# Routed rows fetched and written back by transfers with an address from the index, in a gated mix of a long convolution and a two-row expert

## The chip, the cores and the metric

The kernel runs on one core of one Trainium2 chip. The core has five engines, each with its own instruction stream: TensorE (PE in the profile: matrix products and transposes, results in PSUM), VectorE (DVE), ScalarE (ACT: activation functions, and copies out of PSUM), GpSimd (POOL) and SyncE (SP, which here only issues transfers). Transfers run on 16 DMA engines. Engines wait for each other through semaphores. The metric is the device time of one execution in microseconds (us), the median of several runs.

## What is computed

The input `u` has 2048 tokens of 512 bf16 channels. Two branches are computed from it and mixed per token with a gate.

```
g = sigmoid((u * gate_w).sum(-1))                 # one gate for each token
# branch a: diagonal state-space convolution, one causal filter of 2048 taps for each channel
K[d, l] = Re( sum_n C[d,n] * exp(dt[d] * A[d,n] * l) * dt[d] * B[d,n] ),   l rounded to bf16
a = causal_conv(u, K) + u * Dskip                 # reference: FFT of length 4096
# branch b: the two tokens with the largest router value go through a gated expert
r   = u @ w_r
idx = argsort(-r)[:2]
y   = (silu(u[idx] @ w_gate) * (u[idx] @ w_up)) @ w_down * sigmoid(r[idx])    # 512 -> 1792 -> 512
b   = u;  b[idx] += y
out = g * a + (1 - g) * b
```

Rounding the lag `l` to bf16 makes runs of neighbouring taps equal, so only a few hundred distinct exponents are needed for each channel; a few taps at the two ends of the blocks fall out of this scheme ("edge rows") and are added separately: eight output rows, each a product of taps and a few input rows (tokens 0 to 3, 1024 and 1025).

## The kernel before

Everything is written against one large SBUF array `AR` and four PSUM tensors `ps`; the profile shows these names only. The channels are handled in two halves of 256 (`h` = 0, 1), the tokens in two blocks of 1024.

Stages, in the order in which the program declares them:

- Loads: a constant table `c_bf` (identity matrices first), the parameters, `u` in eight pieces (`U`), the forward matrices `c_fwd`, small constants (`c_rev` is a 128x128 reversal matrix `RV`), the expert's gate and up weights (`WG`, `WU`).
- `scaled`, `trig`, `turns`, `tab1`, `tab2`: tables of complex exponentials, built from products of few direct exponentials and sines (ScalarE for exp and sin, TensorE for the angle steps, L696 to L710; VectorE for the products, L459).
- `routing` (L793 on): transposes `u` (L803), folds the blocks for the forward transform (`fold`, L789), computes gate and router values (`lg`, L819), and finds the two best tokens by two rounds of a maximum over each partition, a TensorE transpose and a maximum across (`gmax`, L848 and L852). This gives a one-hot matrix `OHT` and the token numbers `IDX`. The expert follows: `gat` collects the two rows out of `U` by 64 matmuls with the one-hot matrix (L878) into `XS`; `xed` collects the edge rows with four matmuls against a 0/1 matrix at the end of the constant table (L886) into `XE`; then `ffn1` (L899, gate and up), SiLU, `dn` (L912) and `ytr` (L919), a scaling into `ZB`, and an indirect transfer with accumulation issued by GpSimd (L923) that adds the two rows to `out` in HBM.
- `copies` (two HBM to HBM copies of `u` to `out`, ahead of that scatter), and `reload`, which reads `out` back into `U`: this is `b`.
- `forward` (L954), `kgen` (L973 to L1000: filter taps; its last step multiplies edge taps with `XE` into `ZB`), `kspec` (L1025: filter spectrum, with its matrices `c_ksp`; the second part is seeded either by ScalarE, L1018, or by two matmuls, L1016), `products` (VectorE), `inverse` (L1113), then the scaling and the stores of `out`.

The order is not the order of declaration. `ORDER` is one written-out sequence of all operations; each engine's stream is that sequence restricted to it, and SyncE's transfers are in it too, so a transfer whose wait is not over holds back every transfer behind it in SyncE's stream. `SECOND` says for each operation that may run on two engines (most evictions from PSUM, `EV`, and scalings, `SCL`: ScalarE or VectorE; one step of `trig`, L684; the seed of `kspec`) which one takes it. `PLACES` gives the PSUM banks and SBUF slots. Waits are worked out from what operations read and write. Buffers share memory: the down weights `WD` lie over the transposed `XT`, the filter matrices `KP` over the forward matrices and folded blocks.

The steps named below stand at these lines of the kernel before:

```
gat   L878   64 matmuls 128x2           xed  L886   4 matmuls 40x512
ffn1  L899   2 x 56 matmuls             dn   L912   56 matmuls          ytr  L919
L463  the scaling of the expert's output into ZB;  L923  the scatter;  L931  a clearing that GpSimd does later
L474, L478   EV and SCL;   L684  the int32 step of trig;   L481  every issue of a transfer on SyncE
```

Of the kernel before, what the change touches and what calls it, by code (L numbers as in the profile page):

```python
# [348 lines left out]
EROWS = edge_rows()  # L349
NE = len(EROWS)  # L350
ETB = sorted({PLACE[s][0] for _, _, src in EROWS for s in src})
ERT = sorted({PLACE[t][0] for t, _, _ in EROWS})
EK0 = 256
ECOL = 512
EW = 32 + NE


def small_mats():
    eye = np.eye(128)
    xs = np.zeros((128, len(ETB), EW))  # L360
    ek = np.zeros((128, 4, 2, 32))
    oh = np.zeros((NE, len(ERT) * 128))
    for r, (t, k, src) in enumerate(EROWS):
        for s in src:
            tb, p = PLACE[s]
            xs[p, ETB.index(tb), 32 + r] = 1.0
        for c4 in range(4):
            ek[c4, c4, k, r] = 1.0
        tb, p = PLACE[t]
        oh[r, ERT.index(tb) * 128 + p] = 1.0  # L370
    return np.concatenate([eye, -eye, ek.reshape(128, -1), xs.reshape(128, -1)], 1), oh
# [4 lines left out]
    "02101c01l01h01o00200000101k00300500401j00u00700v00w00600y01201w01u01y00q00h00b00x01301f00z01101g01400n01x00a01000g01m00k02h01p02f01702p06t01v01501t02n"  # L376
    "00902i01800l01901s02d01i02g02q00802o02b01a02z01b00o02e06r02702802c02r00e02j02k02306s00f02l01z03002s02002601e00c01d01r02502m00m03103201q02t05f033034022"
    "05e02u06q00j03509k03e03f02404l06u03g00d03603h03y05h05g05i03i03j09l00s00p03k06v04k03l06w03v03m03n05x05j05w01605k03o03p05l03704m03z03q06x03r01n04500i076"
    "03s07705m02v06y03t07904n02w04o03u03w07007104306z00t07805y04q07b07a07204p05q04r04402907c07307d05r02y07404703x07504s05s02x0b40b304t0b505t04807e04004u04b"
    "0b20b604904a04v07f04d0b705u04e06004104w04c07g0b807h05z06107p0500420ba07j04f0bc05v04x0b906i00r04y0bi06h07k05104g0bd05406j04h0bj07n04i0bl07q05204z07i053"  # L380
    "07o06k07s06l06o06n04607r05505707u05n05607y0bb06p05o05806m05905p0bk05a05b0690bn0be06e06f06g05c06806207w06306a0bf0bm0bg05d06b09m06c06409n06607m06d07t07l"
    "02a0bh08409q07v09o07z03807x0bp0650800bo08109r0c108309p03b06708509t08908208708608a09u0bq09s0br09v08808b08c08d09w03c0bs08e08g08i0bt0bv08f08j0bw0a008l09x"
    "0bz09y08h08x08k08m0a108n0c208y0bu04j0a208v08o08q0a308p08w09z0bx08s08r0a408z0a70by0900a80c308t0a90c40910c60aa0ca0ab0a509c0c00a609a09d09b0ac09h0c508u092"
    "09e09f09g0ad0c70cc0cb0cd0ce09i0930cf0c80cg0c90ci09j0cj0ch0ck0940cm0al0cl0cn0cp0co0cq0cr0cs0am0390950cu0da0db0an03d0cx0ap0ao0960cv0cy0ct0aq0dc0cw0970cz"
    "0980ar0990d00d20d10d40d30d503a0e60de0h10af0ae0d60df0h00e50dg0dh0d70dl0dd0e20do0dm0ag0di0dj0h20dp0dq0dn0dv0fe0dk0ai0dw0d90fg0dr0ds0dt0ah0dx0ff0ak0fj0d8"
    "0fk0e30e40aj0du0as0fh0fp0gy0dz0e10fl0ea0at0eg0e00eo0dy0ge0fi0e70au0e90gz0ep0ev0eh0ee0e80ec0eb0fn0gb0aw0ei0av0fm0gc0gd0ef0gf0ax0et0fo0ay0az0gg0ed0gk0g7"
    "0ey0ej0gj0fq0b10g90ga0eq0es0gi0er0ew0ek0eu0f00ex0g80f10fs0gh0fr0b00ez0f40f80el0ft0f60f50f90em0gp0f70fv0f20gq0fu0gl0en0gr0f30fw0h40fd0fx0gm0fy0gn0fc0h7"
    "0h50gx0h60fa0gs0fb0fz0gv0g00h80ha0gw0g10g30h30h90hb0g20hj0g40hn0g50go0g60hc0ho0hd0he0hk0hl0gu0hp0gt0hm0hf0hg0hq0ht0hu0hh0hr0hi0hs"
)
SECOND = (  # L390
    "000000000000000000000000000000000000000000010000000000000000000000000000000000000000100010001010001000000000100000000000000000000000000000000000000000"
    "000000000000000000001000000100000000000001000000000000000000000000000000000000000000000000001001010000000000000000000000000000000000000000000000000000"
    "000000000000000000000000000000010000001000000000000000000000000000000000000000000000000000000000000000010000000100000000000000000000000000000000000000"
    "000000000000000000000000000000000000100100000010010000000000000000000000000000000000000000000000000000000000000000000000000000000000000000000000000000"
    "0000000000000000000000000000000000000000000"
)
PLACES = (
    "02465433161002423232540160245222227767777201014646000422440404000146624264456404442240101000000000006260260223046640004012343160264022020752457"
# [4 lines left out]
def bass_gated_mix__ssm_conv_s4__moe_arch_mod__prompt_kernel(nc, A_u, A_A_re, A_A_im, A_B_re, A_B_im, A_C_re, A_C_im, A_log_dt, A_Dskip,  # L403
# [9 lines left out]
    rv_c = const(np.eye(128)[::-1], "c_rev")  # L413
# [15 lines left out]
    with ExitStack() as es:  # L429
# [132 lines left out]
        DQ([(CB(0, 128, 0, (1, 256)), cb_c[:, 0:256])], [], [(CB, "i")], 65536)  # L562
# [13 lines left out]
        DQ([(RV(0, 128, 0, (1, 128)), rv_c[:, :])], [], [RV], 32768)  # L576
        DQ([(CF(0, 128, 0, (1, 160)), cf_c[:, :])], [], [CF], 81920)
        DQ([(CB(0, 128, 256, (1, CBW - 256)), cb_c[:, 256:])], [], [(CB, "o")], 196608)
# [10 lines left out]
        TT(DG(0, 128, 0, (128, 4), (1, 128)), CB(0, 128, 0, (0, 4), (1, 128)), DTP(0, 128, 0, (1, 4), (0, 128)), ALU.mult, [CBI, DTP], [DG])  # L589
        AL = psum(2)  # L590
# [205 lines left out]
        def routing():  # L796
# [26 lines left out]
            b = misc()  # L823
            def od(h):
                for par, w in ((0, CB), (1, RV)):
                    r = h.matmul(b(0, 128, 2 * par, (4, 8), (1, 2)), w(0, 128, 0, (1, 128)), SGB(0, 128, 64 + 2 * par, (4, 8), (1, 2)), start=par == 0, stop=par == 1, skip_group_check=True)
                return r
            P.op(PE, od, [(SGB, "p"), CBI, RV], [b], cost=0.06)
            EV(SGB(0, 128, 0, (1, 32)), b(0, 128, 0, (1, 32)), [b.buf], [(SGB, "s")])
# [43 lines left out]
            gb = misc()  # L873
            def gat(h):
                last = None
                for db in range(4):
                    for tb in range(16):
                        last = h.matmul(gb(0, 128, db * 2, (1, 2)), U(0, 128, tb * D + db * 128, (1, 128)), OHT(0, 128, tb * 2, (1, 2)), start=(tb == 0), stop=(tb == 15))  # L878
                return last
            P.op(PE, gat, uk(*range(16)) + [OHT], [gb.buf], cost=64 * 0.0252)  # L880
            EV(XS(0, 128, 0, (1, 8)), gb(0, 128, 0, (1, 8)), [gb.buf], [XS])
            xe = misc()
            def xed(h):
                last = None
                for i, tb in enumerate(ETB):
                    last = h.matmul(xe(0, EW, 0, (1, D)), CB(0, 128, ECOL + i * EW, (1, EW)), U(0, 128, tb * D, (1, D)), start=(i == 0), stop=(i == len(ETB) - 1))  # L886
# [330 lines left out]
```

## Time and profile before

| | |
|---|---|
| median of 3 runs | 149.09 us (148.96 to 149.79) |
| profiled execution | 149.01 us, its span 147.2 us |
| TensorE busy | 139.8 us (95%) |
| VectorE busy | 137.5 us (93%) |
| ScalarE busy | 126.0 us (86%) |
| GpSimd busy | 23.8 us (16%) |
| granted TensorE clock | 1.00 |

The span is the time from the first to the last thing in the trace of one profiled execution; the execution's own time is 1.8 us longer. A line of a page or an answer names the line of the kernel, the engine, the operation, the tiles written and read, and the count; then busy time, mean duration in ns, and the idle time of the engine just ahead of these instructions with what ended it. Durations overlap a little: the next instruction of VectorE or ScalarE begins some 0.07 to 0.1 us before the end of the one ahead. The chain of waits follows back from the last instruction what released it. SPq is SyncE's sequencer, which issues transfers.

### The profile page before, as it was taken

To read this page: it belongs to the slowest core of one execution; us is meant where nothing else is said; L and a number is where in the kernel's file an instruction comes from. 1 tells how busy PE (TensorE), PEld (TensorE's weight loads), DVE (VectorE), ACT (ScalarE), POOL (GpSimd) and SP (SyncE) were. 2 spreads that over 40 slices of the span, in tenths; PEclk is the share of its full clock that TensorE was granted. 3 is DMA by queue.
4 is the path that set the end of the run, shared out by engine and by line. 5 is a ranking of instruction groups with operands and counts; after the bars stand their busy time and mean duration, and the time that the engine had idled before them with its cause. 6 is when DMAs were issued, how large, how long until landed. Compare 5 with 4: busy or idle time off the path is not lost.

```text
span 147.2 us, 4010 instructions
## 1 busy us (share of the span) xinstructions
PE 139.8 (95%) x1731; PEld 102.1 (69%) x1731; DVE 137.5 (93%) x192; ACT 126.0 (86%) x203; POOL 23.8 (16%) x11
## 2 busy tenths in 40 slices
PE   7999999999999999999899999999999999799990
PEld 2766754677564445589768899977866888688870
DVE  0699998999999999999999999999999999999982
ACT  4699999999999999999899999998889998079220
POOL 3001000000000899999000001000000000000000
PEclk9999999999999999999999999999999999999999
DMA  4999999169100000059300006689200004004404
GB/s 121 276 367 298 412 407 558 44 220 533 40 4 0 0 4 0 0 179 414 129 0 4 0 0 206 230 245 390 85 0 4 2 2 143 0 4 140 120 25 143
DMA packets 12787, 21.16 MB, mean 144 GB/s; under 512 B 1207, under 2 KB 8386, under 8 KB 12610
## 3 DMA queue, kind: packets, MB, share of 16 engines
q1 hardware_dynamic: 11762, 20.26, 38.8%
q10 hardware_dynamic: 976, 0.66, 1.5%
q8 instruction: 13, 0.21, 0.6%
q14 instruction: 4, 0.03, 0.1%
q0 software_dynamic: 32, 0.00, 0.0%
HBM read 18.81 MB, written 4.20 MB: 156 GB/s over the span
## 4 chain that ended last, share of the span: by engine, by line
DVE 51%; PE 42%; issue 2%; DMA 2%; SPq 0%; DVEq 0%
DVE AR L459 45%; PE ps L954 19%; PE ps L973 6%; PE ps L705 3%; DVE AR L466 2%; PE ps L899 2%; PE ps L710 2%; DVE AR L474 2%; DMA AR<-c_bf 2%; DVE AR L621 1%; PE ps L1113 1%; PE ps L699 1%; PE ps L878 1%; PE ps L819 1%; PE ps L789 1%
## 5 line engine op out<-in xcount | busy, mean ns | idle before, releaser
L459 DVE TENSOR_TENSOR AR<-AR 128x2048 bf16<-128x2048 bf16 (+7 forms) x133 | 115.5, 927 | 3.5 <-DMA AR<-c_bf 2.8
L474 ACT ACTIVATE AR<-ps 128x1024 bf16<-128x1024 f32 (+6 forms) x66 | 52.6, 833 | 3.1 <-PE ps L1025 2.4
L1113 PE MATMUL ps<-AR 128*128 128x256 bf16 x256 | 29.5, 273 | 0.9 <-DVE AR L459 0.8
L470 ACT ACTIVATE AR<-ps 128x1024 bf16<-128x1024 int16 (+2 forms) x34 | 28.4, 882 | 2.0 <-PE ps L598 1.9
L954 PE MATMUL ps<-AR 128*128 128x512 bf16 x128 | 29.9, 379 | 0.0
L1113 PEld LDWEIGHTS ps<-AR 128*128 128x128 bf16 x256 | 24.5, 98 | 5.2 <-DVE AR L459 2.0
L923 POOL DMA_INDIRECT out_dram<-AR x1 | 21.5, 21527 | 33.9 <-DVE AR L459 33.9
L954 PEld LDWEIGHTS ps<-AR 128*128 128x128 bf16 x128 | 12.1, 97 | 13.6 <-ACT AR L474 0.5
L973 PEld LDWEIGHTS ps<-AR 128*128 128x128 bf16 x512 | 18.6, 96 | 1.8 <-issue 0.5
L973 PE MATMUL ps<-AR 128*128 128x84 bf16 (+1 forms) x512 | 19.0, 196 | 0.4 <-issue 0.4
L1025 PE MATMUL ps<-AR 128*128 128x256 bf16 x160 | 19.3, 273 | 0.1
L1025 PEld LDWEIGHTS ps<-AR 128*128 128x128 bf16 x160 | 15.3, 98 | 4.1 <-DVE AR L459 0.6
L478 ACT ACTIVATE AR<-AR 128x256 int32<-128x256 f32 (+3 forms) x29 | 16.1, 582 | 0.1
L1123 ACT ACTIVATE AR<-ps,AR 128x256 bf16<-128x256 f32 x24 | 10.0, 478 | 4.9 <-PE ps L1113 4.7
L470 ACT ACTIVATE ps<-AR 128x256 f32<-128x256 bf16 x26 | 11.4, 484 | 0.0
L470 ACT ACTIVATE AR<-AR 128x1024 bf16<-128x1024 int16 (+4 forms) x12 | 9.4, 783 | 0.4 <-DVE AR L684 0.3
L646 PE MATMUL ps<-AR 128*128 128x464 bf16 x22 | 6.9, 446 | 0.9 <-DVE AR L649 0.9
L459 DVE TENSOR_TENSOR AR<-AR,ps 128x2048 bf16<-128x2048 bf16 (+1 forms) x6 | 7.2, 1229 | 0.0
L705 PE MATMUL ps<-AR 128*128 128x512 f16 x24 | 6.2, 379 | 0.0
L1135 ACT ACTIVATE AR<-ps,AR 128x256 bf16<-128x256 f32 x2 | 0.9, 474 | 4.8 <-PE ps L1113 4.7
L710 PE MATMUL ps<-AR 128*128 128x512 bf16 x16 | 4.8, 381 | 0.0
L803 PE MATMUL ps<-AR 128*128 128x128 bf16 x64 | 4.4, 219 | 0.3 <-DMA AR<-c_rev 0.2
(76 smaller groups left out, 99.5 us busy)
## 6 DMA issues: line engine op xcount, KB each, us to landing
AR<-c_ksp SPq DMA_DIRECT2D x5, 512.0 KB, 6.1
AR<-in_A_u_dram SPq DMA_DIRECT2D x8, 256.0 KB, 4.8
AR<-out_dram SPq DMA_DIRECT2D x4, 512.0 KB, 4.8
AR<-c_inv SPq DMA_DIRECT2D x1, 2048.0 KB, 8.7
AR<-in_B_w_gate_dram SPq DMA_DIRECT2D x1, 1792.0 KB, 11.6
AR<-in_B_w_up_dram SPq DMA_DIRECT2D x1, 1792.0 KB, 15.2
out_dram<-AR SPq DMA_DIRECT2D x14, 128.0 KB, 2.2
AR<-c_fwd SPq DMA_DIRECT2D x4, 256.0 KB, 6.2
```

Of the source, the lines that this page charges most:

```text
L459: return P.op(DVE, lambda h: h.tensor_tensor(out=o, in0=a, in1=b, op=op), rd, wr, cost=tt_cost(o, a, b), **k)
L470: return P.op(ACT, lambda h: h.activation(out=o, in_=a, func=func, scale=scale, bias=bias), rd, wr, cost=0.185 + nel(o) * 0.833e-3 + (0.09 ...
L474: return P.op((ACT, DVE), (lambda h: h.activation(out=o, in_=a, func=ACTF.Copy), lambda h: h.tensor_copy(o, a)), rd, wr, cost=(0.185 + n * ...
L478: return P.op((ACT, DVE), (lambda h: h.activation(out=o, in_=a, func=ACTF.Copy, scale=c), lambda h: h.tensor_scalar(out=o, in0=a, scalar1= ...
L705: r = hh.matmul(pb(0, 128, b * 512, (1, 512)), TI(4), PC(0, 128, k * D + h * HC, (0, 2), (1, HC)), start=False, stop=True, skip_group_chec ...
L710: r = hh.matmul(pb(0, 128, b * 512, (1, 512)), CB(0, 128, 128 * sign, (1, 128)), TOFF(1), start=False, stop=True, skip_group_check=True)
L923: P.op(POOL, lambda h: h.indirect_dma_start(dr(out, 0, (D, L), (1, D)), bass.IndirectOffsetOnAxis(ap=IDX(0, 2, 0, (1, 1)), axis=0), ZB(0, ...
L954: last = h.matmul(pb(0, 128, j * 512, (1, 512)), F[ft](0, 128, (kt * 2 + 1 - j) * 128, (1, 128)), pm[q](0, 128, kt * 512, (1, 512)), start ...
L973: last = hh.matmul(pb(0, 128, g // k * 512 + g % k * W4 + o, (1, n)), TP[h][1 - i // 2](0, 128, (b0 + g) * 128, (1, 128)), r[i](0, 128, (b ...
L1025: last = hh.matmul(pb(0, 128, n * 256, (1, 256)), KP[u](0, 128, tau * 128, (1, 128)), KC[h](0, 128, jg * 256, (1, 256)), start=(k == 0 and ...
L1113: r = hh.matmul(pb(0, 128, e * 256, (1, 256)), G(0, 128, ((par * 2 + part) * 4 + ft) * 512 + (2 * t2 + e) * 128, (1, 128)), X(0, 128, h * ...
L1123: return [hh.activation(out=U(0, 128, tb * D + h * HC, (1, HC)), in_=pb(0, 128, tb // 2 % 2 * 256, (1, HC)), func=ACTF.Copy, scale=SG(0, 1 ...
```

## The change

- The routed rows are no longer collected by matmuls. When `IDX` is there, SyncE reads each token number from SBUF into a register and issues two transfers from `u` in HBM whose address comes from it: one puts the row as a column pattern into `XS` (128 partitions, 4 values of 2 bytes each), one puts it as a row into `XE`. `gat` and its eviction are gone.
- The expert's output is scaled and added to the fetched row in one VectorE instruction, and SyncE writes the two finished rows to `out` by two transfers with an address from the register, instead of the accumulating scatter on GpSimd. They wait for the two copies, as the scatter did.
- The edge rows' inputs are loaded straight from `u` into `XE` by two small transfers; `xed` and its eviction are gone. There is now one row for each pair of kind and source, and the 0/1 matrix `c_oh` adds up where several sources belong to one output row.
- The reversal matrix is no longer loaded; VectorE copies the identity with its columns read backwards.
- `ORDER`, `SECOND` and `PLACES` are new. Counted over whole streams: TensorE loses `gat` and `xed` and one pair of seed matmuls (ScalarE takes that seed); VectorE gains the reversal copy, has two more 128x256 scalings (ScalarE two fewer), and hands the one int32 step of `trig` it had and one 128x8 eviction to ScalarE. In SyncE's stream the first half of the down weights now stands ahead of the up weights; the fetch stands between the up weights and the second half of the down weights; both copies stand behind that; the row writes stand behind the first filter load, four others behind them; the rest of the constant table is loaded among the filter loads. The first half of the down weights waits for TensorE to finish with `XT`, as before.

```diff
-    xs = np.zeros((128, len(ETB), EW))
     ek = np.zeros((128, 4, 2, 32))
     oh = np.zeros((NE, len(ERT) * 128))
-    for r, (t, k, src) in enumerate(EROWS):
-        for s in src:
-            tb, p = PLACE[s]
-            xs[p, ETB.index(tb), 32 + r] = 1.0
+    for r, (k, _) in enumerate(ESRC):
         for c4 in range(4):
             ek[c4, c4, k, r] = 1.0
+    for t, k, src in EROWS:
         tb, p = PLACE[t]
-        oh[r, ERT.index(tb) * 128 + p] = 1.0
+        for q in src:
+            oh[ESRC.index((k, q)), ERT.index(tb) * 128 + p] += 1.0
...
-        DQ([(RV(0, 128, 0, (1, 128)), rv_c[:, :])], [], [RV], 32768)
...
+        assert ESRC == [(0, 0), (0, 1), (0, BLK), (0, BLK + 1)] + [(1, i) for i in range(4)]
+        for r, src in ((0, ((BLK * D, 2), (D, 2))), (4, ((D, 4),))):
+            DQ([(XE(32 + r, 4, 0, (1, D)), dr(A_u, 0, *src, (1, D)))], [], [(XE, r)], 4096)
...
+        CP(RV(0, 128, 0, (1, 128)), CB(0, 128, 127, (-1, 128)), [CBI], [RV])
...
-            gb = misc()
-            def gat(h):
-                last = None
-                for db in range(4):
-                    for tb in range(16):
-                        last = h.matmul(gb(0, 128, db * 2, (1, 2)), U(0, 128, tb * D + db * 128, (1, 128)), OHT(0, 128, tb * 2, (1, 2)), start=(tb == 0), stop=(tb == 15))
-                return last
-            P.op(PE, gat, uk(*range(16)) + [OHT], [gb.buf], cost=64 * 0.0252)
-            EV(XS(0, 128, 0, (1, 8)), gb(0, 128, 0, (1, 8)), [gb.buf], [XS])
-            xe = misc()
-            def xed(h):
-                last = None
-                for i, tb in enumerate(ETB):
-                    last = h.matmul(xe(0, EW, 0, (1, D)), CB(0, 128, ECOL + i * EW, (1, EW)), U(0, 128, tb * D, (1, D)), start=(i == 0), stop=(i == len(ETB) - 1))
-                return last
-            P.op(PE, xed, uk(*ETB) + [(CB, "o")], [xe.buf], cost=len(ETB) * 0.22)
-            EV(XE(32, NE, 0, (1, D)), xe(32, NE, 0, (1, D)), [xe.buf], [XE])
+            def row(c):
+                return nc.values_load(IDX(c, 1, 0, (1, 1)), engines=[mybir.EngineType.SP], min_val=0, max_val=L - 1, skip_runtime_bounds_check_because="4096 less a match in the table 4096 - token")
+            def gath(h):
+                r = []
+                for c in range(2):
+                    x = A_u[0, bass.ds(row(c), 1), :]
+                    r.append(h.dma_start(XS(0, 128, c, (2, 4)), x.rearrange("o (k p) -> p (o k)", p=128), allow_slow_non_contiguous=True))
+                    r.append(h.dma_start(XE(c, 1, 0, (1, D)), x))
+                return r
+            P.op(SP, gath, [IDX], [XS, (XE, "x")], cost=4.0, n=4, nbytes=1200000, dma=True)
...
-            TS(ZB(0, 2, 0, (1, D)), yt(0, 2, 0, (1, D)), RTS(0, 2, 37, (1, 1)), MUL, [yt, K("rs"), (ZB, None)], [(ZB, "y")])
-            P.op(POOL, lambda h: h.indirect_dma_start(dr(out, 0, (D, L), (1, D)), bass.IndirectOffsetOnAxis(ap=IDX(0, 2, 0, (1, 1)), axis=0), ZB(0, 2, 0, (1, D)), None, compute_op=ADD),
-                 [(ZB, "y"), IDX], [DX], cost=1.5, nbytes=2048, dma=True)
+            STT(ZB(0, 2, 0, (1, D)), yt(0, 2, 0, (1, D)), RTS(0, 2, 37, (1, 1)), XE(0, 2, 0, (1, D)), MUL, ADD, [yt, K("rs"), (ZB, None), (XE, "x")], [(ZB, "y")])
+            P.op(SP, lambda h: [h.dma_start(out[0, bass.ds(row(c), 1), :], ZB(c, 1, 0, (1, D))) for c in range(2)], [(ZB, "y"), IDX], [DX], cost=3.0, n=2, nbytes=2048, dma=True)
```

More of the change, by code (lines that the diff above doesn't have):

```diff
@@ L349 @@
 EROWS = edge_rows()
-NE = len(EROWS)
-ETB = sorted({PLACE[s][0] for _, _, src in EROWS for s in src})
+ESRC = sorted({(k, s) for _, k, src in EROWS for s in src})
+NE = len(ESRC)
 ERT = sorted({PLACE[t][0] for t, _, _ in EROWS})
@@ L379 @@
[L379 to L382, printed above, removed]
@@ new lines @@
+    "000000000000000000010000001000000100000000000000000000000000000000000000000000000000000000001000100000001000000000000000000000000000000000000000000000"
+    "000000000000000000000000000100000000000010000000000000000000000000000000000000000000000000000000011000100000001000000000000000000000000000000000000000"
+    "000000000000000000000000000000000001000000000100100000000000000000000000000000000000000000000000000000000000000000000000000000000000000000000000000000"
+    "000000000010000000000000000000000000000000"
```

46 lines of the change are left out of this document (22 added, 24 removed).

## The prediction

> **What bounds the kernel now.** I read the page's busy shares, then the same engines by stage, then VectorE's waits, then the chain of work in order of time. (In all rows L numbers are lines of the kernel before.)
>
> ```profile
> PE 139.8 (95%) x1731; PEld 102.1 (69%) x1731; DVE 137.5 (93%) x192; ACT 126.0 (86%) x203; POOL 23.8 (16%) x11
> ```
> ```profile
> 3.62:14.40 10.78, 9.97 (x115) 7.39 (x113) 9.55 (x16) 9.38 (x15) 0.55 (x2) 1.00 0.98 312
> 14.40:73.86 59.46, 59.01 (x781) 37.25 (x782) 58.34 (x103) 58.36 (x88) 21.54 (x2) 1.00 0.48 184
> 73.86:139.47 65.61, 64.37 (x798) 53.43 (x799) 65.31 (x65) 55.80 (x99) 0.52 (x1) 1.00 0.26 88
> ```
> ```profile
> DVE AR L464 <- PE ps L598: 1.1, 1, 1.1
> DVE AR L848 <- PE ps L852: 0.6, 2, 0.3
> DVE AR L459 <- PE ps L973: 0.4, 1, 0.4
> ```
>
> (Columns: stretch, its length, busy time of TensorE, of its weight loads, of VectorE, ScalarE and GpSimd, granted clock, DMA share, GB/s.) Three engines are full at once between 14.40 and 73.86: TensorE idles 0.45 us, VectorE 1.12, ScalarE 1.10. From 73.86 to 139.47 VectorE alone is full (0.30 idle) and ScalarE has 9.8 to spare. So VectorE, from 3.62 on, is the line that everything hangs on. A change can win only by shortening VectorE's work or by removing its idle time, 1.23 + 1.12 + 0.30 = 2.65 us before the tail, most of which is waits on TensorE: 1.1 at the start, 0.6 in the routing reductions, 0.4 before the first filter half. The 21.5 us that GpSimd spends in the scatter are on no path: its next user, the reload, is issued at 88.38.
>
> The profiled run took 149.01 us with a span of 147.2, so 1.8 lie outside; the median of the runs, 149.09, is 0.08 above it.
>
> **The change, part by part.** First the stretch of TensorE's order in which the routed rows are handled, then VectorE and ScalarE by shape, the queue, and the transfers' time to landing.
>
> ```profile
> 16.25 1.58 PE ps L819 x64
> 17.83 0.89 PE ps L954 x4
> ...
> 27.02 0.97 PE ps L886 x4
> ...
> 29.73 1.58 PE ps L878 x64
> ...
> 33.06 1.38 PE ps L899 x56
> ```
> ```profile
> 19.21 0.17 DVE L848 TENSOR_REDUCE AR<-AR 128x1 f32<-128x16 bf16 x1
> 33.86 0.13 DVE L464 TENSOR_SCALAR AR<-AR 2x1 int32<-2x1 f32 x1
> ```
> ```profile
> L459 DVE TENSOR_TENSOR AR<-AR 128x2048 bf16<-128x2048 bf16 x22 | 26.5, 1214 | 0.1
> L459 DVE TENSOR_TENSOR AR<-AR 128x1792 bf16<-128x1792 bf16 x18 | 19.2, 1079 | 0.0
> L459 DVE TENSOR_TENSOR AR<-AR 128x512 bf16<-128x512 bf16 x21 | 8.3, 422 | 2.8 <-DMA AR<-c_bf 2.8
> L459 DVE TENSOR_TENSOR AR<-AR,ps 128x2048 bf16<-128x2048 bf16 x4 | 4.8, 1234 | 0.0
> L684 DVE TENSOR_SCALAR AR<-AR 128x1024 int32<-128x1024 int32 x1 | 0.7, 674 | 0.0
> L478 DVE TENSOR_SCALAR AR<-AR 128x256 int32<-128x256 f32 x2 | 0.6, 314 | 0.0
> L463 DVE TENSOR_SCALAR AR<-ps,AR 2x512 bf16<-2x512 bf16 x1 | 0.5, 466 | 0.0
> L466 DVE SCALAR_TENSOR_TENSOR AR<-ps,AR 128x512 f32<-128x512 f32 x1 | 0.7, 692 | 0.0
> L474 DVE COPY AR<-ps 128x8 bf16<-128x8 bf16 x1 | 0.2, 205 | 0.0
> L459 DVE TENSOR_TENSOR AR<-AR 128x256 bf16<-128x256 bf16 x4 | 1.0, 273 | 0.0
> ```
> ```profile
> L684 ACT ACTIVATE AR<-AR 128x1024 int32<-128x1024 int32 x3 | 3.1, 1049 | 0.0
> L478 ACT ACTIVATE AR<-AR 128x256 int32<-128x256 f32 x14 | 5.4, 426 | 0.0
> L474 ACT ACTIVATE AR<-ps 8x512 bf16<-8x512 f32 x1 | 0.6, 588 | 0.0
> ```
> ```profile
> 62.89 2.45 SPq L481 DMA_DIRECT2D AR<-c_ksp  x5
> 88.38 1.88 SPq L481 DMA_DIRECT2D AR<-out_dram  x3
> ```
> ```profile
> AR<-in_B_w_up_dram SPq DMA_DIRECT2D x1, 1792.0 KB, 15.2
> AR<-in_B_w_down_dram SPq DMA_DIRECT2D x1, 768.0 KB, 8.4
> AR<-c_bf SPq DMA_DIRECT2D x1, 104.0 KB, 11.4
> out_dram<-in_A_u_dram SPq DMA_DIRECT2D x2, 13.3
> AR<-in_A_log_dt_dram SPq DMA_DIRECT2D x1, 1.0 KB, 2.2
> ```
> ```profile
> q1 hardware_dynamic: 11762, 20.26, 38.8%
> ```
>
> *TensorE.* Out go the gather of the routed rows (L878, 1.58) and of the edge rows (L886, 0.97): 2.55 us, all in the full stretch. (One pair of carry matmuls, later, goes to ScalarE; it has 9.8 us free there: nothing.)
>
> *VectorE's work.* Out: the 128x1024 int32 step (0.674, now ScalarE's), the 128x8 copy (0.205), the 2x512 scaling (0.466). In: two 128x256 scalings taken from ScalarE (0.314 each, the second in bf16 and bounded by the same row) and a 2x512 multiply-add with a row from PSUM (nearest row 0.692). 1.345 out, 1.320 in: nothing. The reversal copy of 128x128 has no row; nearest are 0.273 for 128x256 and, if walking backwards cost four times that, 1.09. It stands right behind the first scaling, where VectorE waits 1.1 us for L598 anyway: nothing, at both ends. It cannot pay either: the reversal load that it replaces delayed transposes, not VectorE.
>
> *ScalarE in the full stretch.* In: 1.049 (int32 step), about 0.2 (128x8 copy). Out: 0.588 (edge rows), 0.426 (one scaling). Net +0.24 against 1.10 idle: no cost while TensorE feeds it early.
>
> *The fetch.* The index is ready at 33.86 before, 14.65 us behind the first reduction. In the new order that piece lacks, by the rows above, a 128x1792 product (1.08), a 2048 (1.21), four of 512 (1.69), two of 256 (0.55) and the int32 step (0.67), 5.2 in all, and gains another 2048, a fold product (1.23) and a scaling (0.31), 2.75. The first reduction itself comes about 0.3 earlier (the small copy and 0.1 of a narrower product are gone ahead of it): index at 18.9 + 12.2 = 31.1. SyncE then reads two registers and issues four transfers. A register read has no row: nothing is the one end, a SyncE issue (2.45 / 5 = 0.49, the loads of c_ksp) the nearest row; I take that, 0.98 for two, and 4 x 0.49 = 1.96 for the issues; then 2.2 to landing, as of the 1 KB log_dt load. Landed at 31.1 + 0.98 + 1.96 + 2.2 = 36.2. The bound above: a row spread over 128 partitions falls into 512 pieces of 2 bytes, 1024 for two, 64 on each of 16 engines. By the mean packet of q1 (0.388 x 147.2 x 16 / 11762 = 0.078 us) that is 5.0 more, 41.2. log_dt's load (128 pieces of 8 bytes) is the nearest in size, so I take 36.2.
>
> The Trainium skill, page "DMA: Bandwidth & Descriptors", section "Latency and other measured facts", gives a floor of about 600 ns for a register load from memory. With it the fetch would land 0.2 later, at 36.4: an estimate that no run here has shown.
>
> TensorE reaches the first expert product (L899) at 33.06 before. In the new order it has ahead of that, beside the 2.55 removed, 16 more L954 (3.5), six matmuls of the same width for the angles (1.3) and two warming matmuls (0.4): 33.06 + 5.2 - 2.55 = 35.7. So it waits 0.5 for the fetch. TensorE's busy time in the stretch falls to 56.5, 2.1 below ScalarE's 58.6, so it may wait about 2.1 there before anybody else is late: the fetch is free until 37.8 and costs one for one behind that.
>
> *SyncE's queue.* The up weights now stand behind the first down half, which waits for the last reversal of the fold, on TensorE at 16.25 + 1.58 + 16 x 0.22 + about 1.4 of small matmuls = 22.7. Issued at 23.2, landed 15.2 later at the latest, 38.4; their product comes behind the gate's product and eight matmuls of 0.22, at 35.7 + 1.38 + 1.76 = 38.8. Covered by 0.4, and the 15.2 was measured beside the gate weights, which have landed by then. The second down half, behind the fetch, is issued at 34.0 and lands at 42.4 at the latest; its product comes at 38.8 + 1.38 + 3.0 = 43.2. Covered. Both copies of the input to the output go behind that (34.5; 13.3 to landing, 47.8 and some more for the second). The two row writes wait for the copies and stand before four of the five filter loads; those wait for the last forward product anyway (issued at 62.89 before), long after. The tail of the constant table, now among the filter loads, is used behind the first filter half, after 73.86: at 62.9 + 2.0 + 11.4 = 76.3 it would be 2.4 late, but the 11.4 is from the crowded start, and the filter loads are as wanted as it is: I take nothing and keep 2.4. The reload waits for a VectorE instruction near 88 as before.
>
> *Sum.* The two reductions that waited for TensorE (0.6) had a 128x512 and two 128x1024 products to cover the matmul in between, and the edge gather stood ahead of the second matmul; in the new order a fold product (1.23) and a 2048 (1.21) cover them, without L886: the 0.6 goes. The 0.4 before L459 waits for the first half's L973, which stand behind all 2.55 removed: it goes. The 1.1 at the start stays, no gather lies ahead of it. Below that, if the order hides neither, nothing comes; above, all 1.12 + 0.30. What is late next is ScalarE, with 0.86 left. 147.2 - 1.0 + 1.8 = 148.0; in terms of the median 148.1.
>
> **The rivals.**
>
> *ScalarE takes TensorE's place.* Its idle in the stretch falls from 1.10 to 0.86 and VectorE, whose waits on TensorE go, then waits for ScalarE instead. For: it has as little idle as VectorE. Against: part of that idle is itself waiting on TensorE. Then 1.0 comes back: 149.0.
>
> *The fetch is late (slower).* Place: the first expert product; price: landing minus 37.8, on top of the forecast's 148.1, since everything behind that product on TensorE moves and ScalarE and VectorE wait for it. At 41.2 that is 3.4: 151.5. It makes the kernel slower (by over 0.75) from a landing at 39.6 on. For: no row here has 2-byte pieces. Against: log_dt's 2.2.
> The Trainium skill speaks against the change here: "DMA: Bandwidth & Descriptors", section "Rules for kernel authors", says that a last dimension that isn't contiguous becomes one descriptor per element and should be rearranged. By that rule the 1024 pieces are real, and the trace's mean packet prices them at the 5.0 above.
>
> *The constant tail is late.* Up to 2.4 at the first edge taps, of which TensorE's lead takes up some: half of it gives 149.3 to 149.8. For: its place in the queue; against: 104 KB behind loads that are needed right afterwards too.
>
> **How the numbers follow.** Forecast 148.1: 0.45 (0.40 faster by over 0.5%, which is 0.75 us and about what a measurement of this kernel can tell from no change; 0.05 within). ScalarE instead: 0.25 (0.03 faster, 0.20 within, 0.02 slower). Late fetch: 0.22, all slower, most at 150 to 151. Constant tail: 0.08 (0.02 within, 0.06 slower). Together 0.43 faster, 0.27 within, 0.30 slower. The lower bound is all VectorE idle gone except the 1.1 (2.65 - 1.1 = 1.5): 147.6, 147.4 with the spread of the runs; the upper one is the late fetch at 40.5 of its 41.2, 150.8. For the forecast alone 147.5 to 148.6.
>
> **What would show it.** Right: L878 and L886 have no successor on TensorE; VectorE's waits on the reductions and before the first filter half are below 0.2 each; VectorE's busy time is within 0.3 of 137.5; the first expert product starts at 35.5 to 38 without a wait for the fetch. Wrong: TensorE's wait for the fetched rows over 2 us; VectorE's waits reappearing under ScalarE's name; the index later than 32; a register read of over 1 us.

## The result, and the profile after

The changed kernel takes 148.56 us (median of 20 runs), the kernel before, run beside it, 149.35 (20 runs): ratio 0.9949, 95% interval 0.9933 to 0.9965, 0.76 us faster. The forecast was 148.1 in a range of 147.4 to 150.8, with 0.43 for faster by over 0.5%; the interval, 0.5 to 1.0 us, lies on both sides of that 0.5%. The profiled span fell from 147.2 to 146.4. (L numbers below are lines of the kernel that a row comes from. In the changed kernel the products are L455, scalings L474, evictions L470, sines and exponentials L466, forward matmuls L945, angle matmuls L704 and L709, the expert products L891 and the down product L904, the fetch L878 and L879.)

The busy shares of the page, and the same engines by stage (columns as in the prediction; the last stretch ends 0.77 us earlier than before):

```profile
PE 135.5 (93%) x1646; PEld 99.5 (68%) x1661; DVE 137.7 (94%) x193; ACT 126.1 (86%) x202; POOL 2.3 (2%) x10
```
```profile
3.62:14.40 10.78, 9.64 (x110) 7.26 (x109) 9.66 (x17) 9.45 (x15) 0.65 (x3) 1.00 0.99 337
14.40:73.86 59.46, 57.18 (x714) 35.47 (x724) 58.98 (x104) 59.25 (x88) 0.16 (x1) 1.00 0.49 179
73.86:138.70 64.84, 62.08 (x786) 52.53 (x789) 64.37 (x64) 55.00 (x98) 0.53 (x1) 1.00 0.25 86
```

VectorE's waits:

```profile
DVE AR L460 <- PE ps L597: 1.0, 1, 1.0
DVE AR L847 <- PE ps L851: 0.4, 1, 0.4
DVE AR L462 <- PE ps L1104: 0.3, 1, 0.3
```

VectorE's idle time before the tail fell from 2.65 to 1.12 + 0.48 + 0.47 = 2.07 us, and its busy time in the three stretches from 133.20 to 133.01: together the 0.77 (the two ends, 139.47 and 138.70, stand at the same instruction to 0.1 us). In the full stretch TensorE's idle time rose from 0.45 to 2.28, while ScalarE's fell from 1.10 to 0.21.

The gain does not show where the waits went. The first filter product starts on VectorE at 73.85, before at 73.86: in the full stretch the 0.64 us less of idle time is filled with 0.64 us more of work, mostly a 128x2048 product that used to stand behind it (kernel before first, both from 14.40 to 73.86):

```profile
L459 DVE TENSOR_TENSOR AR<-AR 128x2048 bf16<-128x2048 bf16 x17 | 20.5, 1212 | 0.0
```
```profile
L455 DVE TENSOR_TENSOR AR<-AR 128x2048 bf16<-128x2048 bf16 x18 | 21.8, 1208 | 0.0
```

The last stretch, with 64.37 us of VectorE's work instead of 65.31, is the one that gets shorter.

The fetch, in the timeline of VectorE (the index), SyncE (the issues; the second column is the time of one) and TensorE:

```profile
31.02 0.13 DVE L460 TENSOR_SCALAR AR<-AR 2x1 int32<-2x1 f32 x1
31.86 0.40 SPq L878 DMA_DIRECT2D AR<-in_A_u_dram  x1
32.35 0.35 SPq L879 DMA_DIRECT2D AR<-in_A_u_dram  x1
33.40 0.39 SPq L878 DMA_DIRECT2D AR<-in_A_u_dram  x1
33.88 0.34 SPq L879 DMA_DIRECT2D AR<-in_A_u_dram  x1
36.28 1.49 PEld L891 LDWEIGHTS ps<-AR 128*128 128x128 bf16 x56 [0.30 <-DMA AR<-in_A_u_dram]
36.31 1.54 PE L891 MATMUL ps<-AR 128*128 128x2 bf16 x56
```

The index is ready at 31.15; 0.71 later the first transfer is issued, and the second row's transfer, again 0.70 after the issue ahead of it has ended, stands at 33.40. Most of each 0.70 is the read of the token number into the register, which the trace holds too (count; shortest, median and longest in ns; the last two of the four belong to the row writes):

```profile
L873 SPq TENSOR_LOAD <-AR x4: 445/476/484, 31.2 to 56.0; - x4
```

TensorE waits 0.30 and starts the first expert product at 36.31. It waits for all four transfers, since they raise one semaphore and the product waits for its full count; by the trace's records of that semaphore the last of them landed at 36.24.

### The profile page after: what moved, and what is told of

The parts are those of the page before. It is cut to its first block, busy times and chain, and to the rows that moved or that the text cites. A ratio compares the mean times of both kernels' runs of the same rounds, so it can differ in the third digit from the quotient of the medians.

```text
span 146.4 us, 3881 instructions
## 1 busy us (share of the span) xinstructions
PE 135.5 (93%) x1646; PEld 99.5 (68%) x1661; DVE 137.7 (94%) x193; ACT 126.1 (86%) x202; POOL 2.3 (2%) x10
## 4 chain that ended last, share of the span: by engine, by line
PE 67%; ACT 14%; DVE 13%; issue 2%; DMA 2%; SPq 0%; DVEq 0%
PE ps L1104 18%; PE ps L945 15%; PE ps L1016 10%; ACT AR L470 8%; PE ps L964 7%; DVE AR L455 6%; DVE AR L462 3%; ACT AR L474 3%; PE ps L1052 2%; ACT AR L466 2%; DVE AR L470 2%; PE ps L976 2%; DMA AR<-c_bf 2%; PE ps L709 1%; DVE AR L620 1%
## 5 line engine op out<-in xcount | busy, mean ns | idle before, releaser
L455 DVE TENSOR_TENSOR AR<-AR 128x1024 bf16<-128x1024 bf16 (+7 forms) x133 | 115.3, 926 | 3.1 <-DMA AR<-c_bf 2.7
L470 ACT ACTIVATE AR<-ps 128x1024 bf16<-128x1024 f32 (+7 forms) x65 | 51.8, 840 | 4.6 <-PE ps L1016 1.7
L466 ACT ACTIVATE AR<-ps 128x1024 bf16<-128x1024 int16 (+2 forms) x34 | 28.7, 907 | 1.9 <-PE ps L597 1.8
L945 PE MATMUL ps<-AR 128*128 128x512 bf16 x120 | 28.8, 379 | 0.9 <-ACT AR L470 0.5
L1104 PE MATMUL ps<-AR 128*128 128x256 bf16 x256 | 29.3, 273 | 0.1
L945 PEld LDWEIGHTS ps<-AR 128*128 128x128 bf16 x128 | 11.9, 97 | 13.9 <-ACT AR L470 1.1
L1016 PE MATMUL ps<-AR 128*128 128x256 bf16 x160 | 18.8, 273 | 0.0
L474 ACT ACTIVATE AR<-AR 128x256 int32<-128x256 f32 (+3 forms) x27 | 15.4, 597 | 0.1
L1114 ACT ACTIVATE AR<-ps,AR 128x256 bf16<-128x256 f32 x24 | 9.9, 474 | 3.9 <-PE ps L1104 3.6
L466 ACT ACTIVATE ps<-AR 128x256 f32<-128x256 bf16 x26 | 11.3, 483 | 0.0
L466 ACT ACTIVATE AR<-AR 128x1024 bf16<-128x1024 int16 (+4 forms) x12 | 9.3, 788 | 0.0
L455 DVE TENSOR_TENSOR AR<-AR,ps 128x2048 bf16<-128x2048 bf16 (+1 forms) x6 | 7.2, 1213 | 0.0
L704 PE MATMUL ps<-AR 128*128 128x512 f16 x24 | 6.2, 379 | 0.0
L709 PE MATMUL ps<-AR 128*128 128x512 bf16 x13 | 4.1, 382 | 1.4 <-ACT AR L466 1.3
L1052 PE MATMUL ps<-AR 128*128 128x512 bf16 x15 | 3.6, 379 | 1.2 <-ACT AR L474 1.2
L462 DVE SCALAR_TENSOR_TENSOR AR<-ps,AR 128x256 bf16<-128x256 f32 (+2 forms) x8 | 4.1, 538 | 0.5 <-PE ps L1104 0.3
```

The costliest lines, as they stand in the source:

```text
L455: return P.op(DVE, lambda h: h.tensor_tensor(out=o, in0=a, in1=b, op=op), rd, wr, cost=tt_cost(o, a, b), **k)
L462: return P.op(DVE, lambda h: h.scalar_tensor_tensor(out=o, in0=a, scalar=sc, in1=b, op0=op0, op1=op1), rd, wr, cost=0.16 + nel(o) * 1.02e- ...
L466: return P.op(ACT, lambda h: h.activation(out=o, in_=a, func=func, scale=scale, bias=bias), rd, wr, cost=0.185 + nel(o) * 0.833e-3 + (0.09 ...
L470: return P.op((ACT, DVE), (lambda h: h.activation(out=o, in_=a, func=ACTF.Copy), lambda h: h.tensor_copy(o, a)), rd, wr, cost=(0.185 + n * ...
L474: return P.op((ACT, DVE), (lambda h: h.activation(out=o, in_=a, func=ACTF.Copy, scale=c), lambda h: h.tensor_scalar(out=o, in0=a, scalar1= ...
L945: last = h.matmul(pb(0, 128, j * 512, (1, 512)), F[ft](0, 128, (kt * 2 + 1 - j) * 128, (1, 128)), pm[q](0, 128, kt * 512, (1, 512)), start ...
```

## Experiments

The theory: TensorE's 2.55 us of gathers made VectorE wait, and their removal is the gain; the new order is what lets the fetch arrive in time. The rivals: the new order gains by itself, ScalarE becomes the bound, or the fetch costs what it saves. All ratios are to the kernel before, run on the same chip. The changed kernel's 0.9949 is from its own comparison, so a difference to it is a difference of two ratios.

### The two halves of the change

The gathers cut short in the old order (`old_cut`):

```
-                    for tb in range(16):          # gather of the routed rows, start/stop to match
+                    for tb in range(1):
-                for i, tb in enumerate(ETB):      # gather of the edge rows
+                for i, tb in enumerate(ETB[:1]):
```

> The kernel before, in its own order, with the two gathers cut to five matmuls (4 of 64 and 1 of 4; the gathered rows are wrong, all else is computed): about 2.2 us of TensorE's work less, no fetch. My theory, that the gathers made VectorE wait for TensorE: two reductions' 0.6 and the first filter half's 0.4 go, 1.0 us faster, ratio 0.993. Rival, that VectorE's waits go to ScalarE instead or the gain is the new order's: ratio 0.998 to 1.002.

Measured: 0.9968 (0.9939 to 0.9997), 0.5 us faster, between the two. Its full stretch and VectorE's waits:

```profile
14.40:73.86 59.46, 57.17 (x726) 35.82 (x739) 59.07 (x104) 59.14 (x88) 21.52 (x1) 1.00 0.49 183
```
```profile
DVE AR L459 <- ACT AR L474: 0.8, 1, 0.8
DVE AR L466 <- PE ps L1113: 0.5, 1, 0.5
DVE AR L848 <- PE ps L852: 0.3, 1, 0.3
```

VectorE's idle time in the stretch falls from 1.12 to 0.39: one reduction's wait and the first filter half's go, as the theory says. But one wait of 0.8 on ScalarE appears, later than 73.86, about as long as what went: the rival's mechanism, at another place than the prediction put it.

The gathers' time put back in the new order, as wide matmuls at the time where the gather used to stand (`new_wide`, one group of four forward matmuls done four times):

```
-                            for kt in range(4):
+                            for kt in list(range(4)) * reps:   # reps is 4 for one group, else 1
```

> The changed kernel with one group of four wide forward matmuls done four times over at 29.7 us (the gather's old time): 12 matmuls of 0.216 = 2.6 us of TensorE's work, about the 2.55 that the gathers took, without narrow matmuls. My theory, that TensorE's relief is the gain: TensorE has 2.3 us of idle time in the stretch, about 1 of it before the first expert product; the fill uses it up and 0.3 to 1.6 us come back, ratio 0.997 to 1.006. Rival, that the order alone gives the gain: ratio 0.993 to 0.996. The clock should stay at 1.00 here, unlike with the narrow fill.

Measured: 1.0064 (1.0042 to 1.0085), 1.7 us slower than the changed kernel for 2.6 of work; the other 0.9 was slack. VectorE's and ScalarE's waits that came:

```profile
DVE AR L474 <- ACT AR L466: 1.6, 1, 1.6
ACT AR L466 <- PE ps L704: 2.0, 1, 2.0
```

ScalarE waits 2.0 for the angle matmuls behind the added work, and VectorE 1.6 for ScalarE. With TensorE's time put back at this place, the new order is slower than the kernel before, so this order does not gain by itself. The waits that came are not the two that had gone, and the place of the added work has its part in them: the new order with the gathers themselves in it was not run.

The new transfers in the old order (`old_fetch`): the changed kernel's operations with the old list of the order, the fetch behind the index, the edge loads behind the constant tail.

> The new transfers (fetch and row writes with an address from the index, edge rows loaded, reversal copy) in the old order of work. My theory, that the transfers pay only because the order makes room for them: the index comes at 33.9 us as before, the rows land 5.3 later (as in the changed kernel), at 39.1; TensorE reaches the first expert product at 33.1 - 2.55 = 30.5 and waits 8.6, of which about 3 are slack (the 2.55 removed and 0.45 of idle time): 5 to 6 us slower than before, about 154.5, ratio 1.035 to 1.04. Rival, that the transfers carry the gain by themselves and the order is incidental: the wait is hidden, ratio 0.995 or less.

Measured: 1.0478 (1.0409 to 1.0546), 7.2 us slower. The waits, and TensorE's clock in single microseconds (after the length and the busy times of the five engines; then DMA share and GB/s):

```profile
PE ps L891 <- DMA AR<-in_A_u_dram: 6.3, 1, 6.3
DVE AR L455 <- PE ps L891: 7.6, 1, 7.6
```
```profile
37.00:38.00 1.00, 0.00 (x0) 0.00 (x0) 1.00 (x2) 0.00 (x0) 0.00 (x0) 1.00 0.16 2
38.00:39.00 1.00, 0.00 (x0) 0.00 (x0) 0.39 (x1) 0.00 (x0) 0.00 (x0) 0.55 0.33 46
43.00:44.00 1.00, 0.95 (x3) 0.40 (x3) 0.00 (x0) 1.00 (x2) 0.00 (x0) 0.50 1.10 353
44.00:45.00 1.00, 1.00 (x26) 0.72 (x25) 0.00 (x0) 0.97 (x2) 0.00 (x0) 0.54 2.98 1210
```

TensorE waits for the rows, and from 38.1 to 44.9 the granted clock is 0.50: the expected 5 to 6 us, and 1 to 2 more that no step had. That the clock makes up these is not separated from the wait. In the old order, which has no room for them, the transfers do not pay.

### The price of a late fetch

Six more register reads written ahead of the fetch (`late6`):

```
                 r = []
+                for _ in range(6):
+                    row(0)
```

> The changed kernel with six more reads of the index register ahead of the fetch, and nothing else. A read and its issue took about 0.7 us to the first issue, so six delay the fetch by up to 4.2, landing at 40.5 instead of 36.3. My step, fetch free until 37.8 and one for one behind that: 2.7 us slower than the changed kernel, ratio 1.013. Rival A, no slack since VectorE and ScalarE are full: 4.2 slower, ratio 1.023. Rival B, the expert products are on no path: no change, ratio 0.995. If a read costs less than 0.3, the landing stays ahead of 38 and nothing is seen.

Measured: 0.994 (0.9912 to 0.9969), as the changed kernel. The index (31.20 to 31.33 here) is followed by the first issue at 32.05, the same 0.72 behind its end as without the edit. But the six reads are not among what ran: this run's trace holds four register reads, as the changed kernel's does.

```profile
L873 SPq TENSOR_LOAD <-AR x4: 442/478/487, 31.4 to 56.8; - x4
```

So the run says nothing about the price of a late fetch, and nothing against the read as the main part of the 0.7. In the changed kernel the first read takes 0.47 of it (31.18 to 31.65 in the trace), and the instructions that form the address and the gaps between them the 0.21 up to the issue at 31.86.

The fetch made to wait for a later VectorE product (`late_dep`):

```
+        P.ops[149].deps.add(171)     # operation 149 is the fetch, 171 the product
```

> The changed kernel with the fetch made to wait for a fold product that ends on VectorE at about 34.05 instead of for the index at 31.15: everything of the fetch 2.9 us later, landing at 39.2. My step, free until 37.8 and one for one behind it: 1.4 slower than the changed kernel, ratio 1.004. Rival A, no slack at all: 2.9 slower, ratio 1.014. Rival B, the expert products are on no path: ratio 0.995. If TensorE's clock falls in the 3.2 us of waiting and narrow work, 1 to 2 us come on top.

Measured: 1.0277 (1.0223 to 1.0332), 4.9 us slower than the changed kernel. ScalarE's timeline, and the clock:

```profile
38.76 1.07 ACT L466 ACTIVATE AR<-AR 128x1024 bf16<-128x1024 int16 x1
40.52 0.19 ACT L470 ACTIVATE AR<-ps 128x28 bf16<-128x28 f32 x1 [0.70 <-PE ps L891]
44.41 0.19 ACT L470 ACTIVATE AR<-ps 128x28 bf16<-128x28 f32 x1 [1.65 <-PE ps L891]
```
```profile
41.00:41.50 0.50, 0.50 (x4) 0.26 (x3) 0.50 (x1) 0.50 (x1) 0.00 (x0) 0.93 1.86 799
41.50:42.00 0.50, 0.50 (x3) 0.21 (x2) 0.50 (x2) 0.50 (x3) 0.00 (x0) 0.50 0.00 0
47.00:48.00 1.00, 1.00 (x3) 0.30 (x2) 1.00 (x3) 1.00 (x3) 0.00 (x0) 0.50 0.00 0
48.00:49.00 1.00, 1.00 (x5) 0.45 (x4) 1.00 (x2) 0.68 (x2) 0.00 (x0) 0.87 0.00 0
```

The product starts at 38.94. The first engine to wait for it is ScalarE, by 0.70, when it evicts the product. So a start up to 38.94 - 0.70 = 38.2 would have been free by these rows, against the prediction's 37.8; in the changed kernel the product ends at 37.85 and is evicted at 39.73 without a wait, which gives the same. But TensorE had been without work for 2.5 us and then had 1.4 us of matmuls two columns wide, and its clock is at half from 41.4 to 48.3. The second wait of 1.65 and those behind it fall in that time. Of the 4.9 us, 0.7 is the landing behind 38.2; the rest falls in the time of the halved clock. That the clock alone makes up the rest is worked out from these rows, not measured by a run at a full clock.

The Trainium skill, page "TensorE: Matmul & The Clock Gate", Part 1 on the clock gate, says that the clock is halved after an idle window of about 3.4 us, and that these windows run freely. This trace agrees on their length: 41.4 to 48.3 is two of them. It does not show such a window without work: TensorE had idled for 2.5 us.

The gathers' time put back as narrow matmuls shows the same without a wait for a transfer (`new_fill`, 64 matmuls of two columns and 4 of 512 ahead of the first product):

```
+                def fill(h, bb=bb):           # 64 of (128x128)x(128x2), then 4 of (128x40)x(128x512)
+                    ...
+                P.op(PE, fill, [*F, OHT, CBI], [bb.buf], cost=2.5)
```

> The changed kernel with 64 narrow and 4 wide matmuls (the gathers' 2.55 us, on other operands, result overwritten) put back into TensorE's order seven operations ahead of the first expert product. My theory, that TensorE's relief is the gain: the stretch from 14 to 74 us has 2.3 us of TensorE idle, so the fill makes it full again and 0.3 to 1.0 us come back, ratio 0.997 to 1.002. Rival, that the new order gives the gain by itself: ratio stays 0.993 to 0.996.

Measured: 1.022 (1.0163 to 1.0278), 4.0 us slower than the changed kernel, far over both. Clock rows and ScalarE's wait:

```profile
38.00:38.50 0.50, 0.50 (x4) 0.20 (x4) 0.50 (x2) 0.04 (x1) 0.00 (x0) 0.82 5.01 2105
38.50:39.00 0.50, 0.50 (x3) 0.13 (x1) 0.50 (x2) 0.00 (x0) 0.00 (x0) 0.50 0.61 262
40.00:41.00 1.00, 1.00 (x3) 0.32 (x3) 1.00 (x5) 0.00 (x0) 0.00 (x0) 0.50 2.53 999
41.50:42.00 0.50, 0.50 (x25) 0.50 (x23) 0.50 (x2) 0.50 (x1) 0.00 (x0) 0.77 0.35 131
```
```profile
ACT AR L470 <- PE ps L954: 3.3, 1, 3.3
```

Behind a gap of 0.6 us and 1.8 us of matmuls of two columns the clock is at 0.50 from 38.3 to 41.7, although the records show TensorE mostly busy, and ScalarE waits 3.3 for the forward matmuls that stand in that time. That the narrow matmuls count as little or no activity is a reading of this run and the one before; it was not separated from the gap. Narrow matmuls alone do not do it: the 64 of the router values (L818, 15.7 to 17.4 us in the changed kernel) pass at a clock of 1.00. So this run tests the theory badly, and `new_wide`, at a clock of 1.00, takes its place.

### Pieces and the reversal matrix

Pieces of 8 bytes instead of 2 (`contig`):

```
-  h.dma_start(XS(0, 128, c, (2, 4)), x.rearrange("o (k p) -> p (o k)", p=128), allow_slow_non_contiguous=True)
+  h.dma_start(XS(0, 128, 4 * c, (1, 4)), x.rearrange("o (p k) -> p (o k)", p=128))
-  W(db, fb), XS(0, 128, db * 2, (1, 2))
+  W(db, fb), XS(0, 128, db, (4, 2))
```

(and both weight loads with rows 4p to 4p+3 on partition p.)

> The changed kernel with the expert input laid out so that each partition takes four neighbouring elements: 256 pieces of 8 bytes instead of 1024 of 2 bytes for the two rows (the gate and up weights are loaded in the matching order, one contiguous 14 KB run a partition). My step, that the landing goes by the fixed time of a transfer (2.2 us, as of the log_dt load) and not by the pieces: the rows land within 0.3 of 36.3, time as of the changed kernel, ratio 0.993 to 0.997. Rival, one descriptor per element sets the landing: it comes 1 us or more earlier; TensorE's wait of 0.3 for it goes and the time falls by up to 0.3, ratio 0.992 to 0.994.

Measured: 0.9959 (0.9927 to 0.9992), as the changed kernel. The packets of q1 (changed kernel first):

```profile
q1 hardware_dynamic: 12696, 20.22, 39.3%
```
```profile
q1 hardware_dynamic: 11160, 20.22, 39.2%
```

1,536 packets go, 768 of which are the fetch's. The product starts at 36.74, without a wait on a transfer, so its start does not tell when the rows landed. The trace's records of the fetch's semaphore do: all four transfers had landed at 36.24 in the changed kernel and at 35.47 here, 2.84 and 1.74 us behind the issue of the second column row (33.40 and 33.73), and 5.1 and 3.9 us behind the index. So the pieces of 2 bytes cost about 1.1 us of the landing, as the rival had it, and TensorE's wait of 0.3 goes. Whether the time falls by up to that 0.3 cannot be told: the interval holds both expectations.

The Trainium skill's rule of one descriptor per element (page "DMA: Bandwidth & Descriptors", section "Rules for kernel authors") agrees with the count of packets: the changed kernel's trace has 1024 packets of 2 bytes.

The reversal matrix alone, in the old order (`old_rev`):

```
-        DQ([(RV(0, 128, 0, (1, 128)), rv_c[:, :])], [], [RV], 32768)
+        CP(RV(0, 128, 0, (1, 128)), CB(0, 128, 127, (-1, 128)), [CBI], [RV])   # behind the first scaling
```

> The kernel before, in its own order, with the reversal matrix copied on VectorE behind the first scaling, and its load left out of SyncE's queue; nothing else. My step: nothing, since VectorE waits 1.1 us there anyway, ratio 0.998 to 1.002. Rival A, a copy that walks backwards costs over 1.1: ratio above 1.002. Rival B, the load left out lets the transposes start earlier and takes the wait at the start: ratio 0.995 to 0.998.

Measured: 0.9994 (0.996 to 1.0028): nothing, within 0.4%. The copy's row, in the changed kernel:

```profile
L464 DVE COPY AR<-AR 128x128 bf16<-128x128 bf16 x1 | 0.2, 188 | 0.0
```

### Which engine is next

Two products made cheaper (`dve_less`), and the same with one int32 step given back to VectorE (`act_less`):

```
         def TT(o, a, b, op, rd, wr, **k):
+            if len(P.ops) in (170, 171):
+                return P.op(DVE, lambda h: h.tensor_scalar(out=o, in0=a, scalar1=1.0, scalar2=None, op0=ALU.mult), rd, wr, **k)
```

> The changed kernel with two 128x2048 products (of two operands, 1.21 each) replaced by scalings of one operand (about 0.67 each), at 31 to 34 us, so part of the computation is wrong: VectorE has 1.1 us less to do, ScalarE and TensorE the same. My reading, that VectorE is the line that everything hangs on: 0.9 to 1.1 faster than the changed kernel, ratio 0.988. Rival, that ScalarE with 0.21 us of idle time in the stretch is now level with it: at most 0.3 faster, ratio 0.993 to 0.995.

(`act_less` adds one flipped bit of `SECOND`, operation 254, which sends the int32 step to VectorE.)

> The same two scalings, and one 128x1024 int32 step of ScalarE (1.05) moved to VectorE (0.67), as it was in the kernel before: VectorE has 0.4 us less, ScalarE 1.05 less than in the changed kernel. My reading: the gain is VectorE's, 0.3 to 0.5, ratio 0.991 to 0.993, less than with the two scalings alone. Rival, ScalarE level with VectorE: 0.5 to 1.0 faster, ratio 0.988 to 0.991, more than with the scalings alone.

Measured: `dve_less` 0.9912 (0.9885 to 0.994), 0.55 us better than the changed kernel's 0.9949 for 1.1 less work, though the intervals overlap a little; `act_less` 1.0208 (1.0164 to 1.0252). VectorE's new wait of the first, then the waits of the second:

```profile
DVE AR L457 <- ACT AR L468: 0.5, 1, 0.5
```
```profile
DVE AR L685 <- ACT AR L468: 2.0, 1, 2.0
ACT AR L468 <- DVE AR L457: 2.9, 1, 2.9
PE ps L711 <- ACT AR L468: 2.7, 3, 1.7
```

The first stands between the two theories: about half of the 1.1 that VectorE saves comes back as a wait of 0.5 for ScalarE. The second missed both. The int32 step (L685) at its place in VectorE's queue waits 2.0 for ScalarE, then ScalarE waits 2.9 for VectorE, whose products stand in between, and TensorE, which waits 1.7 in one piece, has a clock of 0.50 for 3.4 us from 48.4 on (mean in the stretch 0.97). So `act_less` does not measure ScalarE's load; it shows that the choice of engine belongs to the order.

The last scaling given to ScalarE (`late_flip`, one bit of `SECOND`), and this with pieces of 8 bytes and both expert rows issued first (`best`):

```
+  x = [A_u[0, bass.ds(row(c), 1), :] for c in range(2)]
+  r = [h.dma_start(XS(0, 128, 4 * c, (1, 4)), x[c].rearrange("o (p k) -> p (o k)", p=128)) for c in range(2)]
+  r += [h.dma_start(XE(c, 1, 0, (1, D)), x[c]) for c in range(2)]
```

> The changed kernel with its last scaling of 128x256 (0.28 on VectorE at 139.9) given to ScalarE, which is idle there. VectorE sets the end: 0.2 to 0.28 faster than the changed kernel, ratio 0.993. TensorE's last inverse matmuls set it: no change, ratio 0.995.

> The pieces of 8 bytes, both rows for the expert products issued ahead of both rows for the output, and the last scaling on ScalarE. The second row's issue comes about 0.5 earlier, at 32.9 instead of 33.4, so TensorE's wait of 0.3 for the rows goes. If a little slack on TensorE is worth something: 0.3 to 0.5 faster than the changed kernel, ratio 0.991 to 0.993. If VectorE and ScalarE are both full there: as the changed kernel with its last scaling moved, ratio 0.993 to 0.995.

Measured: 0.9936 (0.991 to 0.9963) and 0.992 (0.9894 to 0.9945). Both are below the changed kernel's 0.9949, and both intervals overlap with its own, so neither is shown to beat it. In `best` all four transfers had landed at 35.05 and the product started at 36.62 without a wait for them, so the 0.3 went there too. At the end TensorE takes up most of what VectorE gives: VectorE's last wait, 0.3 in the changed kernel, is in `late_flip`

```profile
DVE AR L462 <- PE ps L1104: 0.5, 1, 0.5
```

## Why the prediction was right, and where it was not

**The gain.** Right in sign, and in size within the noise: 1.0 forecast, 0.8 measured in the span and 0.76 in the medians (0.5 to 1.0). That it came so near is in part luck. The sum was VectorE's idle time ahead of the tail alone, of which 1.0 was to go and 0.58 went. The rest, about 0.2, had been put at nothing: VectorE's work that went from ahead of the tail into it, where VectorE has idle time (one of the two scalings, 0.28, now stands at 139.93, and the tail is no longer for it, 7.70 against 7.73). In cause right in the main: taking the gathers out gains a little in the old order (`old_cut`, 0.5 with an interval from 0.04 to 0.9), and putting their time back into the new one loses more than the gain (`new_wide`). How much of the 0.76 is the order's is not shown.

**VectorE's waits.** The wait before the first filter half went, though that half starts no earlier; the one at the start stayed at 1.0. Of the two reductions' 0.6, 0.4 stayed. The step that failed is "a fold product and a 2048 cover them": it looked at VectorE's cover and not at what stands ahead of the reduction's matmul on TensorE.

```profile
22.15 3.62 PE L945 MATMUL ps<-AR 128*128 128x512 bf16 x15
25.63 0.46 PE L851 MATMUL ps<-AR 128*128 128x128 f32 x2
```

Fifteen forward matmuls in a row stand there, and the transposing matmul comes behind them at 25.63.

**VectorE's work.** 137.7 against 137.5, within the 0.3. The copy took 0.19, less than the nearest row of the prediction (0.27 for 128x256), so walking backwards cost nothing that shows.

**ScalarE in the stretch.** The term "+0.24 against 1.10 idle" was too small: ScalarE was busy 59.25 there instead of 58.60. The term counted what changes its engine and not what the new order moves: the total hardly rose (126.0 to 126.1), and work came forward out of the last stretch (55.8 to 55.0). The rival that had ScalarE take TensorE's place was half right: in the changed kernel VectorE names no wait for it over 0.2, but a VectorE with 1.1 less to do loses about half of that to it (`dve_less`).

**The fetch.** Index at 31.15 for 31.1; four issues done at 34.22, 3.07 behind it, for 2.94; landing at 36.24 for 36.2; first product at 36.31 for 36.2, the 35.7 and a wait of 0.5. The register reads were right, 0.47 and 0.48 for 0.49 each. An issue took 0.34 to 0.40 instead of 0.49, and the instructions and gaps between reads and issues, about 0.64 in all, made up for that. The Trainium skill's floor of about 600 ns for a register load (page "DMA: Bandwidth & Descriptors", section "Latency and other measured facts") is above what this trace shows: the four reads, from SBUF, took 445 to 484 ns. That the landing fits is in part luck. With pieces of 8 bytes it came 1.0 us behind the last issue (`contig`, 34.45 to 35.47), not the 2.2 of the log_dt load; the pieces of 2 bytes, put at nothing, brought it back to 2.0. The 5.0 at the mean packet's price did not come: the pieces cost about 1.1.

**Free until 37.8, one for one behind it.** The threshold came out near (38.2 by the rows of `late_dep`), but not for the prediction's reason: it was taken from TensorE's idle time in the whole stretch, and what set it there is the place in ScalarE's order where the product is evicted. The price did not hold. A landing at 38.9 cost 4.9 instead of 1.1, and the clock fell behind the wait. The late-fetch rival's 151.5 for 41.2 was by that too cheap.

**The queue.** First down half issued at 22.35 (22.7), second at 34.28 (34.0), down product at 44.3 (43.2), none late. The constant tail was issued at 64.80 and landed 5.4 later, at 70.2 instead of 76.3: the 11.4 of the crowded start did not carry over, and that rival fell.

**What stays open.** How much the new order is worth without the transfers was not measured apart from them. What takes the clock down, the gap, the narrow matmuls or both, was not separated.

## What to carry to other kernels

Work taken off a full engine is worth what the waits for it and the next engine's idle time allow: here 2.55 us off TensorE gave 0.8, since VectorE had only 1.0 of such waits and ScalarE little idle time left. When a wait is to go, look at what stands ahead of its releaser in that engine's own queue, not only at what covers it on the waiting side. Two rows fetched with an address from the index need a place in the order, here 5.1 us from index to landing with pieces of 2 bytes and 3.9 with pieces of 8, and a wait in front of narrow matmuls can cost more than its length, since TensorE's clock may halve behind it.

## What the runs showed of the hardware that was not expected

- TensorE's clock fell to 0.50 for 3.4 us behind a gap of 0.6 us and 1.8 us of matmuls two columns wide (`new_fill`), and for 6.8 us behind a wait of 2.5 us and 1.4 us of such matmuls (`late_dep`). In the changed kernel a wait of 0.3 and the same 1.4 us of narrow matmuls passed at 1.00.
- A transfer with an address from a register is issued 0.70 to 0.72 us behind the index, or behind the issue ahead of it; 0.47 to 0.49 of that is the read of the register (changed kernel and `late6`).
- Two rows of 512 pieces of 2 bytes had landed 2.84 us behind the second one's issue; with 128 pieces of 8 bytes a row it was 1.74 (`contig`). The kernel's time did not change by more than the noise.
- A 128x128 copy in reversed column order took 0.188 us on VectorE.
